# A convolution feeding two MLPs on one Trainium2 core: an instruction order written out in full, with the convolution moved to the second MLP's stretches

## The chip, the cores and the metric

The kernel runs on one core of one Trainium2 chip. The metric is the time of one execution in microseconds (us) of device time; the time before is the median of three runs.

## The reference, cut to what matters

`x` has 4 sequences of 4096 tokens with 192 channels; each of 8 heads (24 channels) has a softmaxed filter of 7 taps. Two MLPs follow, 192 to 2048 to 192, on the 16384 tokens. `x` and the filter come in float32, the MLPs' weights in float64, which the kernel turns into float32 with integer operations.

```python
w = softmax(weight)                        # 8 heads x 7 taps
out = einsum('hk,bskhg->bshg', w, x_unf)   # causal convolution over the tokens
h = out @ w_in1;  z = (h * cos(h)) @ w_out1
h = z @ w_in2;    y = where(h > 0, h, exp(min(h, 0)) - 1) @ w_out2
```

## The kernel before, in words

Channels lie on partitions, tokens in the free dimension. The 16384 tokens are 32 **blocks** of 512, and four blocks make a **group**. A group goes through the first MLP (32 steps, here a *stretch of MLP 1*), then through the second (a *stretch of MLP 2*), so that the activation table changes twice a group. A block has 16 hidden tiles of 128 x 512; a **step** is two of them (`u` and `v`), eight steps a block, 512 steps in all. The list `steps` says which block and which pair comes when; before, the first two blocks of the first stretch are interleaved there with a lag of three steps (`SKEW`).

Each number is split into a high and a low part, and products are made of high x low, low x high and high x high. A step has these parts:

- `emit_A` (L501, matmuls L509): 18 matmuls of 64 rows make `u` and `v` in PSUM; two matmuls, one on each half of the array's rows, run at a time. PSUM has two buffers for `u`, two for `v`.
- For each of the two tiles an element chain. MLP 1: `emit_act1` (ACT L517, the whole number of turns), `emit_mid` (DVE L528, the fraction), `emit_act2` (ACT L534, sine), `emit_g` (DVE L542, the product). MLP 2: ACT L519, ACT L536, DVE L544. The last of them frees the PSUM buffer. Then `emit_hi` (ACT L550, `gh`) and `emit_lo` (POOL L555, `gl`) split the result.
- `emit_B` of the step two before (`LAG`, L558, matmuls L574, in the first two blocks L571): 20 matmuls of 64 rows into four accumulators `a0, b0, a1, b1`, which have one buffer each. At a block's end `evac` (L576) empties them: ACT copies two (L587), DVE two (L591), and `sums` (L597) adds the pairs on POOL (L602, L606), folds a half onto the other (ACT L604, POOL L608), and splits the result for MLP 2 (ACT L612, L615, POOL L614, L617) or transposes and stores it (DVE L628, L631).

`element(q)` (L748) writes one tile at a time: sine of tile q-1, first ACT operation of tile q, product of q-1, `mid` of q, split of tile q-2.

Three streams are fed in between the steps, each a generator that is called a number of times per step:

- `convs()` (L687): the convolution of the coming blocks, for the 128 lower channels (`"a"`) of each block and for the 64 upper channels (`"c"`) of two blocks at once. One `conv` (L334) is eight calls with one DVE operation each: a transpose (L342), a first tap (L354), six more taps (L356, with two inputs in SBUF). Block 0's upper channels and block 1 are made by TensorE (`conv_by_products`, L395, matmuls L405). Three buffers hold its results for the lower channels (`YA`).
- `prepare()` (L636): the decoding of both MLPs' weights. An item of 128 x 256 numbers is a load, ACT and DVE operations (L178 to L184), an add on POOL (L186), and a split (ACT L218 or L239, POOL L220 or L241). `need` (L681) drives it until the weights that a step wants are there.
- `chores`: `sums`, `begin_split` (L721, the split of the next block's convolution, which first drives `convs()` until that block is there) and `double_z`, one call at each half of a step.

In `step` (L766) `convs()` is called once a step in MLP 1 and twice in MLP 2, but not where a chore has run. The order of the first 48 steps (`FREE`) is set by a scheduler, from there on the code's order is the engines' order.

## Time and profile before

| | |
|---|---|
| runs | 2497.09, 2501.37, 2496.46 us (median 2497.09) |
| profiled execution | 2503.75 us, its span 2502.0 us |
| PE busy | 2368.6 us (95%), weight loads 1948.2 us (78%) |
| ACT busy | 1886.8 us (75%) |
| POOL busy | 1735.9 us (69%) |
| DVE busy | 1626.5 us (65%) |
| mean granted TensorE clock | 0.970 |

The first row is what a change is measured by; the second belongs to the one execution from which all rows of the trace come. A busy share is a mean over stretches of different kinds, so it is read stretch by stretch. Matmuls overlap their neighbours, so the time from one matmul's start to the next one's start says more than one matmul's length. "Idle before" is the time that an engine stood still just before an instruction, with what ended it.

### The profile page before, as it was taken

The numbers are of one execution on the slowest core, as the hardware profiler recorded it, in microseconds if no ns is written. First come the engines' busy times: TensorE is split into PE (matmuls) and PEld (weight loads), VectorE is DVE, ScalarE is ACT, GpSimd is POOL, SyncE is SP. The second block draws the span as 40 slices with busy tenths as digits, with TensorE's granted clock in tenths as the row PEclk, the third lists the DMA queues.
The fourth block names the chain that finished last, engine by engine and source line by source line (L and its number), as shares of the span: only waits on it lengthen the run. The fifth ranks groups of instructions, "written<-read, shape, count | busy, mean of one in ns | idle before, by whom it ended". The sixth has DMA issues, their size and how long they took to land.

```text
span 2502.0 us, 51010 instructions
## 1 busy us (share of the span) xinstructions
PE 2368.6 (95%) x19426; PEld 1948.2 (78%) x19426; DVE 1626.5 (65%) x2341; ACT 1886.8 (75%) x3527; POOL 1735.9 (69%) x1395
## 2 busy tenths in 40 slices
PE   7987999899999999999999999999999999999998
PEld 4655888788887888878887788787887878887886
DVE  8689456776567755776557865677556775577533
ACT  5565878678787787777777787777878777777876
POOL 6467777567776677666777677767766767766775
PEclk8797999999999999999999999999999999999999
DMA  5023121211221122212121212121122112211111
GB/s 157 5 60 100 32 46 33 55 41 24 59 53 24 41 47 43 47 27 57 34 59 25 63 24 53 37 47 41 26 57 53 24 40 53 43 35 38 31 31 31
DMA packets 279782, 112.14 MB, mean 45 GB/s; under 512 B 231920, under 2 KB 246512, under 8 KB 279536
## 3 DMA queue, kind: packets, MB, share of 16 engines
q1 hardware_dynamic: 279216, 108.62, 20.1%
q8 instruction: 152, 2.49, 0.4%
q14 instruction: 94, 0.77, 0.1%
q10 hardware_dynamic: 320, 0.26, 0.0%
HBM read 30.18 MB, written 12.58 MB: 17 GB/s over the span
## 4 chain that ended last, share of the span: by engine, by line
PE 61%; DVE 19%; ACT 8%; POOL 4%; issue 4%; DMA 1%; SPq 1%; POOLq 0%; DVEq 0%; ACTq 0%
PE a L574 28%; PE u L509 25%; DVE y L356 6%; DVE w L528 5%; DVE w L542 4%; PE v L509 4%; PE b L574 3%; ACT w L534 3%; POOL gl L555 2%; ACT w L517 1%; ACT w L536 1%; ACT w L519 1%; ACT gh L550 1%; DVE y L354 1%; PE a L571 1%
## 5 line engine op out<-in xcount | busy, mean ns | idle before, releaser
L555 POOL TENSOR_TENSOR gl<-w,gh 128x512 fp32r<-128x512 f32 x1024 | 1347.2, 1320 | 701.0 <-ACT gh L550 564.6
L574 PE MATMUL a<-gh,wo_hl 64*128 64x512 f32 x1984 | 620.4, 393 | 66.3 <-ACT w L534 37.7
L550 ACT ACTIVATE gh<-w 128x512 fp32r<-128x512 f32 x1024 | 640.2, 626 | 22.7 <-DVE w L542 13.4
L574 PE MATMUL b<-gh,wo_hl 64*128 64x512 f32 x1984 | 620.2, 393 | 0.4 <-DVE e L591 0.3
L574 PEld LDWEIGHTS a<-gh,wo_hl 64*128 64x128 f32 x1984 | 365.9, 186 | 137.6 <-ACT w L534 48.4
L534 ACT ACTIVATE w<-w 128x512 f32<-128x512 f32 x512 | 321.6, 630 | 175.0 <-DVE w L528 173.8
L544 DVE SCALAR_TENSOR_TENSOR w<-w,u 128x512 f32<-128x512 f32 x256 | 176.1, 688 | 409.2 <-ACT w L536 399.7
L509 PE MATMUL u<-ch,wi_c 64*128 64x512 f32 x1024 | 404.1, 395 | 0.0
L509 PE MATMUL v<-ch,wi_c 64*128 64x512 f32 x1024 | 403.0, 394 | 0.7
L574 PE MATMUL a<-gl,wo_hl 64*128 64x512 f32 x992 | 395.6, 399 | 8.2 <-POOL gl L555 7.3
L509 PE MATMUL u<-sh,wi_o 64*128 64x512 f32 x1024 | 400.8, 391 | 1.7 <-DMA sh<-xh 1.7
L509 PE MATMUL v<-sh,wi_o 64*128 64x512 f32 x1024 | 400.4, 391 | 0.0
L574 PE MATMUL b<-gl,wo_hl 64*128 64x512 f32 x992 | 394.9, 398 | 0.0
L574 PE MATMUL a<-gh,wo_s 64*128 64x512 f32 x992 | 389.4, 393 | 0.0
L574 PE MATMUL b<-gh,wo_s 64*128 64x512 f32 x992 | 388.9, 392 | 0.0
L574 PE MATMUL a<-gl,wo_s 64*128 64x512 f32 x992 | 388.2, 391 | 0.0
L574 PE MATMUL b<-gl,wo_s 64*128 64x512 f32 x992 | 387.9, 391 | 0.0
L574 PEld LDWEIGHTS b<-gh,wo_hl 64*128 64x128 f32 x1984 | 365.0, 186 | 10.9 <-DVE e L591 0.7
L536 ACT ACTIVATE w<-w 128x512 f32<-128x512 f32 x512 | 318.7, 626 | 0.9
L356 DVE SCALAR_TENSOR_TENSOR y<-xT,wch,y 128x512 f32<-128x512 f32 x276 | 308.2, 1117 | 1.6
L519 ACT ACTIVATE w<-u 128x512 f32<-128x512 f32 x256 | 152.7, 596 | 173.6 <-PE v L509 117.2
L544 DVE SCALAR_TENSOR_TENSOR w<-w,v 128x512 f32<-128x512 f32 x256 | 176.0, 687 | 127.1 <-ACT w L536 121.7
(150 smaller groups left out, 7207.3 us busy)
## 6 DMA issues: line engine op xcount, KB each, us to landing
out_dram<-e SPq DMA_DIRECT2D x192, 64.0 KB, 1.9
xa<-in_x_dram SPq DMA_DIRECT2D x112, 88.0 KB, 2.7
sh<-xh SPq DMA_DIRECT2D x64, 128.0 KB, 2.4
sl<-xl SPq DMA_DIRECT2D x64, 128.0 KB, 2.3
cl<-zc SPq DMA_DIRECT2D x64, 128.0 KB, 2.3
ch<-zc SPq DMA_DIRECT2D x64, 128.0 KB, 2.4
sl<-zl SPq DMA_DIRECT2D x64, 128.0 KB, 2.3
sh<-zh SPq DMA_DIRECT2D x64, 128.0 KB, 2.3
```

The source lines that it names most:

```text
L354: nc.vector.tensor_scalar(out=o, in0=i, scalar1=w, scalar2=None, op0=ALU.mult)
L356: behind[0] = nc.vector.scalar_tensor_tensor(out=o, in0=i, scalar=w, in1=o, op0=ALU.mult, op1=ALU.add).ins
L509: led[0] = nc.tensor.matmul(u[i], lhsT=at, rhs=x[k + h][p], start=n == 0, stop=n == len(ops) - 1).ins
L519: nc.scalar.activation(out=w, in_=u, func=AF.Relu, scale=-1.0)
L528: paced[0] = nc.vector.scalar_tensor_tensor(out=w, in0=u, scalar=0.25, in1=w.bitcast(I32), op0=ALU.add, op1=ALU.subtract).ins
L534: nc.scalar.activation(out=w, in_=w, func=AF.Sin, scale=6.283185)
L536: nc.scalar.activation(out=w, in_=w, func=AF.Exp, scale=-1.0)
L542: nc.vector.tensor_tensor(out=w, in0=u, in1=w, op=ALU.mult)
L544: paced[0] = nc.vector.scalar_tensor_tensor(out=w, in0=w, scalar=-1.0, in1=u, op0=ALU.add, op1=ALU.max).ins
L550: nc.scalar.activation(out=gh, in_=wrk[s], func=AF.Copy)
L555: nc.gpsimd.tensor_tensor(out=gl, in0=wrk.pop(s), in1=f32(gs[s][0]), op=ALU.subtract)
L574: nc.tensor.matmul(a[o + i], lhsT=w[p, f, :], rhs=g[p], start=first, stop=final)
```

## The change

1. **Element steps two tiles at a time.** The function `element` goes. A step writes `act1` of both tiles, `mid` of both, then twice: split of one tile of the step before, `act2` and `g` of one tile of this step.
2. **Convolution in MLP 2's stretches alone.** `convs()` is called twice in each step of MLP 2, whether or not a chore has run, and not in MLP 1 (a third call in each step of the first group's MLP 2 stretch, once the weights are decoded). A fourth buffer holds the lower channels' results, so that a whole group's convolution can be made ahead. Blocks 2 and 3 of the first group are made by TensorE (lower channels).
3. **Blocks in single file.** The interleaving of blocks 0 and 1 goes, and with it their matmuls of 128 rows (L571).
4. **Decoding by step.** The decoding is called four times in each of the first eight steps, then once a step. Its first ACT operation is always ACT's for MLP 1 (before, every other time DVE's). During the first eight steps one PSUM bank holds a tile of the decoding, so that `v` has one buffer there.
5. **Accumulators.** ACT copies `a0` and `a1`, and DVE adds `b0` and `b1` to the copies as it reads them from PSUM; the two adds on POOL (L602, L606) go.
6. No order is set by a scheduler any more.

```diff
-            both = 2 if (m, b0) == (1, 0) else 0
-            if both:
-                for j in range(NP + SKEW):
-                    steps += [(m, b, j - b * SKEW) for b in range(both) if 0 <= j - b * SKEW < NP]
-            steps += [(m, b, j) for b in range(b0 + both, b0 + GROUP) for j in range(NP)]
+            steps += [(m, b, j) for b in range(b0, b0 + GROUP) for j in range(NP)]
...
-        u = [ps_h.tile([P, N], F32, tag=f"u{i}", name="uv"[i]) for i in (0, 1)]
+        spare_bank = banks and s % 2 == 0
+        u = [ps_h.tile([P, N], F32, tag="u0", name="u"), (banks[0] if spare_bank else ps_h).tile([P, N], F32, tag="u1", name="v", bufs=1)]
...
-        for i in (1, 3):
-            if a[i] is not None:
-                nc.scalar.activation(out=e[i], in_=a[i], func=AF.Copy, scale=scale)
-        yield
...
+        for i in (0, 2):
+            nc.scalar.activation(out=e[i], in_=a[i], func=AF.Copy, scale=scale)
+        yield
+        for i in (0, 2):
+            nc.vector.scalar_tensor_tensor(out=e[i], in0=a[i + 1], scalar=scale, in1=e[i], op0=ALU.mult, op1=ALU.add)
+        chores.append(sums(m, b, e))
+        yield
...
+        for b in range(ROWS, NBLK):
+            while b - GROUP not in split_done:
                 yield
             yield from conv("a", b)
-            if b >= ROWS and b % 2 == 0:
+            if b % 2 == 0:
                 yield from conv("c", b)
             conved.add(b)
...
     def step(s):
...
+        if s == NP:
+            need(1, NF, "oh", "os")
+            top.close()
+            banks.append(ctx.enter_context(tc.tile_pool(name="ps_u", bufs=1, space=bass.MemoryType.PSUM)))
+        pair_of = lambda k: (2 * k, 2 * k + 1) if 0 <= k < total else ()
+        now, old = pair_of(s), pair_of(s - 1)
+        calls = 0 if prepared else CALLS if s < NP else 1
+        if now:
             m, b, j = steps[s]
             need(m, j + 1, 0, 1, "c")
             emit_A(s)
-        element(2 * s, None)
+        for q in now:
+            emit_act1(q)
+        for q in now:
+            emit_mid(q)
...
         for i in (0, 1):
-            if i:
-                element(2 * s + 1, finish)
-            next(prep, None)
-            if not chore():
-                if s < FREE:
-                    with tc.issue_after(paced[0]):
-                        next(cq, None)
-                elif s >= total or steps[s][0] == 2 or i == 0:
-                    next(cq, None)
+            if calls > i:
+                next(prep, None)
+            if old:
+                emit_hi(old[i])
+                emit_lo(old[i])
+            if now:
+                emit_act2(now[i])
+            next(finish, None)
+            if now:
+                emit_g(now[i])
+            busy = chore()
+            if s < NP:
+                for _ in range(EARLY // 2):
+                    next(cq, None)
+            elif len(conved) < GROUP or s >= total or steps[s][0] == 2:
+                next(cq, None)
+        for _ in range(calls - 2):
+            next(prep, None)
+        if prepared and NP * GROUP <= s < 2 * NP * GROUP:
+            next(cq, None)
```

Where the order moves. First, DVE in the fourth stretch of MLP 1, eleven steps before its end (`w<-u,w` and `w<-v,w` at L528/L524 are `mid` of the two tiles, at L542/L538 the products; L356 is a tap of the convolution, L460/L463 the split of the next block). Before:

```order
L528 SCALAR_TENSOR_TENSOR w<-u,w 128x512
L356 SCALAR_TENSOR_TENSOR y<-xT,wch,y 128x512 x5
L342 STREAM_TRANSPOSE xT<-xa 128x704
L542 TENSOR_TENSOR w<-u,w 128x512
L528 SCALAR_TENSOR_TENSOR w<-v,w 128x512
L460 TENSOR_TENSOR xl<-y,xh 128x512
L542 TENSOR_TENSOR w<-v,w 128x512
```

Now:

```order
L524 SCALAR_TENSOR_TENSOR w<-u,w 128x512
L524 SCALAR_TENSOR_TENSOR w<-v,w 128x512
L538 TENSOR_TENSOR w<-u,w 128x512
L463 TENSOR_TENSOR xl<-y,xh 128x512
L538 TENSOR_TENSOR w<-v,w 128x512
```

Five taps and a transpose stood between a tile's `mid` and its product; no operation of the convolution is left there, and the two `mid` stand together.

Second, ACT in the step of the same stretch that empties the accumulators (`e<-b` or `e<-a` is the copy out of an accumulator, `gh<-w` the split). Before:

```order
L517 ACTIVATE w<-u 128x512
L550 ACTIVATE gh<-w 128x512
L534 ACTIVATE w<-w 128x512
L517 ACTIVATE w<-v 128x512
L587 ACTIVATE e<-b_14035 128x512
L587 ACTIVATE e<-b_14037 128x512
L550 ACTIVATE gh<-w 128x512
L534 ACTIVATE w<-w 128x512
```

Now:

```order
L515 ACTIVATE w<-u 128x512
L515 ACTIVATE w<-v 128x512
L546 ACTIVATE gh<-w 128x512
L530 ACTIVATE w<-w 128x512
L574 ACTIVATE e<-a_14159 128x512
L574 ACTIVATE e<-a_14161 128x512
L546 ACTIVATE gh<-w 128x512
L530 ACTIVATE w<-w 128x512
L585 ACTIVATE e<-e 64x512
```

Between `mid` of a tile and its sine (L534/L530) ACT now has the other tile's first operation and a split to do; the copy of the half (L585) follows in the same step, since it no longer waits for POOL.

Third, DVE in a step of MLP 2 that empties the accumulators (L591 reads one accumulator, L577 adds one to ACT's copy of the other). Before:

```order
L544 SCALAR_TENSOR_TENSOR w<-w,u 128x512
L591 TENSOR_SCALAR e<-a_15058 128x512
L591 TENSOR_SCALAR e<-a_15060 128x512
L544 SCALAR_TENSOR_TENSOR w<-w,v 128x512
L544 SCALAR_TENSOR_TENSOR w<-w,u 128x512
```

Now:

```order
L540 SCALAR_TENSOR_TENSOR w<-w,u 128x512
L347 STREAM_TRANSPOSE xT<-xa 128x704
L577 SCALAR_TENSOR_TENSOR e<-b_15163,e 128x512
L577 SCALAR_TENSOR_TENSOR e<-b_15165,e 128x512
L540 SCALAR_TENSOR_TENSOR w<-w,v 128x512
L358 TENSOR_SCALAR y<-xT,wch 128x512
```

An operation of the convolution now stands ahead of the reads that free the accumulators, and another behind the second tile's product.

## Rows read from the trace of the kernel before

**Rows 1.** The page's first part: busy time and share of each engine.

```profile
PE 2368.6 (95%) x19426; PEld 1948.2 (78%) x19426; DVE 1626.5 (65%) x2341; ACT 1886.8 (75%) x3527; POOL 1735.9 (69%) x1395
```

**Rows 2.** Windows by stretch: from:to, us, busy PE PEld DVE ACT POOL, clock, DMA.

```profile
423.30:585.90 162.60, 145.69 (x1222) 128.30 (x1218) 127.25 (x174) 117.84 (x217) 105.94 (x83) 0.96 0.19 38
...
1021.50:1178.80 157.30, 147.62 (x1222) 125.99 (x1218) 118.78 (x162) 118.03 (x216) 105.62 (x83) 0.97 0.16 35
1178.80:1318.00 139.20, 138.54 (x1216) 113.32 (x1216) 75.69 (x110) 111.03 (x211) 102.12 (x79) 1.00 0.25 50
...
2202.40:2355.90 153.50, 145.26 (x1214) 121.36 (x1212) 108.89 (x154) 118.00 (x216) 105.41 (x83) 0.98 0.17 38
```

**Rows 3.** Timeline of DVE and PE where a block ends; last row, a tap elsewhere.

```profile
1059.04 1.74 DVE L356 SCALAR_TENSOR_TENSOR y<-xT,wch,y 128x512 f32<-128x512 f32 x1
1061.90 1.27 DVE L591 TENSOR_SCALAR e<-a 128x512 f32<-128x512 f32 x2
1062.72 0.47 PE L574 MATMUL a<-gh,wo_hl 64*128 64x512 f32 x1 [1.79 <-ACT w L534]
1064.30 0.62 PE L574 MATMUL a<-gh,wo_hl 64*128 64x512 f32 x1
1064.73 0.62 PE L574 MATMUL a<-gh,wo_hl 64*128 64x512 f32 x1
...
1206.94 0.75 DVE L356 SCALAR_TENSOR_TENSOR y<-xT,wch,y 128x512 f32<-128x512 f32 x1
```

**Rows 4.** Timeline of DVE and PE at the five taps in a row.

```profile
1117.82 4.84 DVE L356 SCALAR_TENSOR_TENSOR y<-xT,wch,y 128x512 f32<-128x512 f32 x5
1124.90 0.61 PE L574 MATMUL a<-gh,wo_hl 64*128 64x512 f32 x1 [2.87 <-ACT gh L550]
```

**Rows 5.** Groups by line in the MLP 1 stretch 1021.5 to 1178.8 (busy us, mean ns).

```profile
L356 DVE SCALAR_TENSOR_TENSOR y<-xT,wch,y 128x512 f32<-128x512 f32 x17 | 23.8, 1401 | 0.1
L528 DVE SCALAR_TENSOR_TENSOR w<-u,w 128x512 f32<-128x512 f32 x31 | 21.2, 684 | 4.6 <-ACT w L517 4.2
L587 ACT ACTIVATE e<-b 128x512 f32<-128x512 f32 x8 | 4.3, 596 | 0.0
L536 ACT ACT_TABLE_LOAD x1 | 1.3, 1283 | 0.0
```

**Rows 6.** The same in the MLP 2 stretch 1178.8 to 1318.

```profile
L555 POOL TENSOR_TENSOR gl<-w,gh 128x512 fp32r<-128x512 f32 x65 | 85.9, 1325 | 38.6 <-ACT gh L550 31.3 <-issue 4.8 <-PE b L574 1.5
L356 DVE SCALAR_TENSOR_TENSOR y<-xT,wch,y 128x512 f32<-128x512 f32 x19 | 16.9, 891 | 0.0
```

**Rows 7.** Windows of the first group: steps 0-2, 3-7, 8-15, 16-23, 24-31, 32-39, 40-63.

```profile
26.50:76.20 49.70, 40.04 (x127) 23.98 (x125) 44.33 (x83) 30.67 (x74) 38.17 (x46) 0.77 0.27 79
76.20:110.20 34.00, 34.00 (x128) 23.78 (x129) 14.40 (x22) 18.29 (x35) 12.69 (x12) 0.78 0.00 1
110.20:158.50 48.30, 44.92 (x239) 31.72 (x238) 35.98 (x56) 33.38 (x61) 28.87 (x24) 1.00 0.21 55
158.50:237.10 78.60, 55.96 (x321) 40.60 (x321) 74.00 (x122) 44.65 (x95) 56.24 (x59) 0.81 0.30 84
237.10:276.40 39.30, 36.27 (x273) 27.81 (x271) 24.85 (x42) 31.44 (x59) 29.13 (x27) 0.91 0.26 53
276.40:312.80 36.40, 35.93 (x300) 29.34 (x298) 12.96 (x20) 30.33 (x56) 27.51 (x22) 1.00 0.11 25
312.80:417.80 105.00, 104.31 (x914) 89.69 (x912) 57.47 (x83) 81.65 (x154) 74.14 (x57) 1.00 0.23 45
```

**Rows 8.** The same windows for the decoding's line L183 alone (one per item).

```profile
26.50:76.20 49.70, 10.37 (x20) 0.77 0.27 79
...
158.50:237.10 78.60, 8.73 (x20) 0.81 0.30 84
```

**Rows 9.** Groups by line over the span: the convolution on TensorE, all 128 rows.

```profile
L405 PE MATMUL y<-rows 128*128 128x512 f32 (+1 forms) x8 | 5.8, 878 | 0.0
```

**Rows 10.** Windows: the first eight steps of the stretch that starts at 1021.5.

```profile
1021.50:1058.20 36.70, 35.24 (x312) 31.32 (x310) 28.66 (x41) 28.61 (x54) 24.97 (x20) 1.00 0.19 40
```

More of the change, by code (lines that the diff above doesn't have):

```diff
@@ L22 @@
 GROUP = 4
-HID = 2
 LAG = 2
@@ L304, in from_rows @@
         p = slice(0, D2 if alone else P)
[L305 removed]
+        ps = [ps_a.tile([P, N], F32, tag=ACC[i], name="xps") if b < 2 and (alone or b == 1) else ps_h.tile([P, N], F32, tag="u0", name="xps") for i in range(2)]
         for o, k0, c, np in ((ps[0], KM, KH, 2 * Q), (ps[1], 0, KM, P)):
@@ L332, in from_rows, with y_tile @@
         return xT
+    def y_tile(what, b):
+        if what == "a" and b >= GROUP and b % GROUP == GROUP - 1:
+            return later[0].tile([P, N], F32, tag="y", name="y")
+        return yp.tile([P, N], F32, tag="y" + what, name="y", bufs=YA if what == "a" else 2)
     def conv(what, b):
@@ L406, in conv_by_products @@
             yield
+        if what == "a" and b > 1:
+            y = y_tile(what, b)
+            nc.scalar.activation(out=y, in_=o, func=AF.Copy)
+            o = y
         ys[what, b] = o
     xTs = {}
-    behind = [None]
-    tiled = [True]
-    def one_by_one():
-        return tc.issue_after(behind[0]) if behind[0] is not None and tiled[0] else nullcontext()
     def tokens(*order):
@@ L560, in emit_B @@
         h, l, sel = (wo[m, n] for n in ("h", "l", "s"))
-        whole = m == 1 and b < 2
         if j == 0:
-            acc[m, b] = [ps_a.tile([P, N], F32, tag=n, name=n) for n in (ACC[b::2] if whole else ACC)]
+            acc[m, b] = [ps_a.tile([P, N], F32, tag=n, name=n) for n in ACC]
         a = acc[m, b]
@@ L820, in conv_then_two_mlps @@
         need(1, 1, 0, 1, "c")
-    for s in range(FREE):
-        step(s)
-    tiled[0] = False
-    with tc.manual_schedule():
-        for s in range(FREE, total + LAG):
+        for s in range(total + LAG):
             step(s)
```

140 lines of the change are left out of this document (49 added, 91 removed).

## The prediction

> **What bounds the kernel now.** The page's first part comes first: PE is busy for 95% of the span, the others for 65 to 75% [rows 1]. A mean over unlike stretches cannot say what 5% of idle PE is worth, so the windows come next, cut where the MLPs change [rows 2]. A stretch of MLP 2 takes 139.2 us with PE busy for 138.5 of them at the full clock: nothing else can bound it. A stretch of MLP 1 has the same 32 steps and takes 162.6, 157.3 and 153.5 us in the rows shown. The seven stretches of MLP 1 and the six of MLP 2 between them fill 423.3 to 2355.9 us, 1932.6 us; with six times 139.2 taken out, the seven take 1097 us, 156.8 each, 18 us above the floor that MLP 2 shows. There PE is idle for 10 us and its mean clock is 0.96 to 0.98.
>
> The timeline says where. At a block's end a tap of the convolution takes 1.74 us on DVE (it overlaps a POOL operation there; the shortest ones take 0.75, last row), the reads that empty the accumulators therefore start at 1061.90, and the next block's first output matmul waits 1.79 us; then pairs of matmuls start 0.43 us apart (1064.30, 1064.73) instead of 0.23, since the clock fell to its lower level [rows 3]. Once a group `begin_split` drives five taps at once, 4.84 us on DVE, and PE stands for 2.87 us [rows 4]. So DVE's order is the bound of MLP 1, not DVE's amount of work. The first group is a case by itself: its 64 steps take 391.3 us, where PE's pace would need 278 [rows 7].
>
> **The change, part by part.** Durations are from the profiled execution, 2503.75 us (span 2502.0, 1.75 around it), which stands 6.7 above the median of the runs; that comes off at the end.
>
> *Stretches of MLP 1, groups 2 to 8.* The 17 taps in the stretch shown cost 23.8 us of DVE [rows 5]. Without them DVE has 95 us of work, ACT still 118, POOL less than 105 (two adds a block go), all under PE's 138.5 [rows 2]. The new order also takes away ACT's wait for `mid`: between a tile's `mid` (0.68) and its sine ACT has another 0.59 and 0.63 us to do. What could still hold PE is the block's end: copies and reads ran side by side, now DVE's add comes after ACT's copy. After the block's last matmul: copy 0.60 [rows 5], add 0.68 (taken from L528, which also reads one operand in PSUM [rows 5]) with 0.1 between them, so the first pair of accumulators is free after 1.4 us and the second after some 2.1. PE has nine pairs of `emit_A` in between, 9 x 0.2275 = 2.05 us (138.5 us / 608 pairs = 0.228), and needs the second pair 0.46 later still. It just fits; I take 0.4 us a block for the operations that may stand ahead of the add, and 1 us for the table load of 1.28 [rows 5]. A stretch then takes 138.5 + 1 + 4 x 0.4 = 141 us, seven take 987: **-110**. Bounds: 139.2 as MLP 2 now (-123), and 36.7 per eight steps, which is what the fastest block end-to-end shows now with three taps in it [rows 10], 147 a stretch (-68).
>
> *Stretches of MLP 2.* 17 taps come in at 0.89 us [rows 6], 15 us, and some four first taps and transposes, at a tap's price 4 more: DVE goes from 75.7 to some 95, far below 138.5. They hide beside PE as the 19 taps there do now. Not hidden is one at a block's end: convolution is now called whether or not a chore runs, so a tap stands ahead of the adds (third place of the order). With 0.75 us ahead, the first pair is free after about 2.2 us and not 1.4, against 2.05: 0.1 to 0.5 us; with 1.74 ahead, 1.1. I take 0.5 us, three times a stretch (the convolution is done after 24 of 32 steps), six stretches: **+9**. Bounds 0 and the second rival. The last stretch has no convolution and stays.
>
> *The first group* [rows 7], by pieces:
> - Steps 0 to 7 take 83.7 us now, 49.7 of them with 20 items of decoding [rows 8] and DVE busy for 44.3. The same items come in the first six steps. To those 44.3 come four operations of 0.68 for each of five more steps (14) and eight of the convolution (7): 65 us, at the same 89% share 73. `v` has one buffer, so a step's matmuls wait for the last product of the step before; I take 80. Bounds 70, and 110 if the clock stays low all through as it does from steps 2 to 5 now (mean 0.77 and 0.78).
> - Steps 8 to 15: 48.3 us now; eight steps at 4.35, seven products of the convolution at 0.88 [rows 9] and 5 us of waits make 46. Bounds 41 and 55.
> - Steps 16 to 31: 117.9 us now, since 20 items fall into seven steps with DVE busy for 74 of 78.6. One call a step makes it 0.6 items a step: DVE needs 2.2 us an item (the 74 less 22 for the elements and some 8 for convolution and splits, over 20), so 4 x 0.68 + 0.6 x 2.2 = 4.05 us a step, just below PE, with POOL and ACT near it too; I take 4.85 a step, 78 us. Bounds 70 and 95.
> - Steps 32 to 39: 36.4 us now. Some ten items are left, and `need` drives them just before the matmuls that use them: 48. Bounds 36 and 58.
> - Steps 40 to 63: 105.0 us now; three operations of the convolution a step for 16 steps make DVE's 4.7 us a step: 109. Bounds 104 and 115.
>
> Together 361 against 391: **-30**, bounds -70 and +42.
>
> Sum: -110 + 9 - 30 = -131; 2503.75 - 131 = 2372.75, less 6.7: 2366, say **2367 us**, for the median.
>
> **The rivals.**
> 1. *MLP 1 keeps half of its loss.* ACT and POOL carry the splits and `sums` in a bunch after each block's end, and 36.7 us stands for eight steps even where PE does not lose its clock. 147 us a stretch, 42 more: 2409. Against it: ACT's 118 us leave 20 free. 14%.
> 2. *The taps cost MLP 2 more.* If each of 36 taps takes 1.74 us as where it meets POOL [rows 3], 24 of 32 steps need 2 x 0.69 + 1.5 x 1.74 + 0.7 = 4.7 us of DVE against 4.33: 9 us a stretch, and the adds at three block ends come 1.3 us late with 1.6 us of low clock behind, 9 more: 6 x 18 less the 9 counted is 99 more, 2466. Against it: at two taps a step the taps there average 0.89 now [rows 6]. 6%.
>    The Trainium skill (SBUF — State Buffer, "Who interferes with whom") says that a VectorE instruction with two SBUF inputs and a GpSimd instruction that reads SBUF share a port, and that whichever comes second is blocked for the other's whole length. Rows 3 agree (1.74 against 0.75 us). By that rule at its worst each tap waits out one whole split of 1.32 us [rows 6], an estimate of 2.07 us a tap, some 20 us a stretch besides the block ends, and the time would be near 2530 (1%, in the last 2% below).
> 3. *The first group grows.* With every piece at its upper bound it is 42 longer, not 30 shorter: 2439. For it: one buffer for `v`, products on PE, low clock. Against it: DVE's bunch in steps 18 to 24 goes. 5%.
> 4. *Slower: the accumulators come free too late.* The one mechanism is copy, then add, then the next block's first matmul. It decides from 2.05 us after the last matmul on: if a wait of 0.7 us or more regularly stands before the add (ACT still in a sine when the block ends, a tap on DVE), PE pays at all 64 block ends what it pays in rows 3: 1.79 idle and eight pairs at 0.2 more, 3.4 us, 218 us in all. Less the 20 counted, 198 more: 2565. Against it: in MLP 1 nothing but products and `mid` stands there. 3%.
>
> That the change doesn't do what it says is excluded for MLP 1 by the order itself: no operation of the convolution stands between its steps. What it can't exclude, 2%.
>
> **How the numbers follow.** The forecast's own case has 70%, within 2335 to 2400 (the bounds of the first group, mostly). The range reaches down to 2325 for a first group at its best, and up to 2430 to take in rival 1 and part of rival 3; that leaves out under 2 in 10. About 0.2%, 5 us, is what a measurement here can tell from no change. Faster: the forecast, rivals 1 and 3 and most of 2, 94%. Same 2%. Slower: rival 4 and a little else, 4%.
>
> **What would show it.** In the changed profile the windows of the seven MLP 1 stretches should be 139 to 143 us, with no gap of PE above 1 us and the clock at 1.00; DVE's busy time should be about 92 to 95 us in either kind of stretch, ACT's wait for `mid` near nothing. The MLP 2 stretches should be 140 to 142 us, with what is lost at the three block ends that have a tap ahead of the adds. The 64 first steps should take some 360 us, the first eight about 80, with the granted clock the doubtful row. Wrong would be a stretch of MLP 1 above 147 us, PE waiting for the adds (L577) at each block's end, or a first group that is no shorter.

## The result, and the profile after

The change takes 2459.14 us in the median of four runs (2452.73 to 2463.16), the kernel before beside it 2497.49 (four runs): a ratio of 0.9841, with an interval from 0.9815 to 0.9867. That is 1.6% faster, where 5.2% were forecast, and outside the range. The profiled execution took 2456.48 us (span 2454.8). Against its counterpart of before, 2503.75, the sum of the prediction stood at 2372.75; so 84 us have to be found.

The page's first part, busy time and share by engine, hardly differs from [rows 1]; GpSimd alone has clearly less to do:

```profile
PE 2342.7 (95%) x19614; PEld 1896.1 (77%) x19614; DVE 1612.3 (66%) x2314; ACT 1860.3 (76%) x3544; POOL 1607.1 (65%) x1273
```

The windows by stretch answer to [rows 2] (from:to, length, busy PE, PEld, DVE, ACT, POOL, granted clock, DMA): a stretch of MLP 1, the stretch of MLP 2 behind it, and the last one of MLP 2, which has no convolution.

```profile
1011.90:1151.30 139.40, 139.25 (x1223) 117.46 (x1221) 92.75 (x140) 114.18 (x216) 95.11 (x74) 1.00 0.15 34
1151.30:1301.50 150.20, 144.93 (x1217) 115.97 (x1215) 102.95 (x132) 111.23 (x210) 97.07 (x71) 0.99 0.26 52
...
2308.40:2442.80 134.40, 133.78 (x1170) 108.80 (x1168) 50.81 (x76) 105.64 (x201) 87.14 (x70) 1.00 0.12 26
```

MLP 1 is at TensorE's pace: 139.4 us, 139.25 of them busy, at the full clock. MLP 2 has become the slow one: 150.2 us, TensorE idle for over 5. The last stretch, 134.4 against 134.1 before, shows that without convolution the new order costs MLP 2 nothing. From the first split of a stretch to that of the next, the seven MLP 1 stretches take 139.7 us in the mean (156.7 before), the six MLP 2 stretches 149.9 (139.3 before).

The blocks of that MLP 2 stretch, in the same columns:

```profile
1151.30:1189.30 38.00, 35.81 (x306) 29.32 (x304) 31.09 (x37) 27.84 (x54) 27.93 (x20) 1.00 0.24 47
1189.30:1225.80 36.50, 35.61 (x307) 28.41 (x305) 28.60 (x37) 26.99 (x52) 23.68 (x17) 1.00 0.32 61
...
1262.40:1301.50 39.10, 37.79 (x308) 29.88 (x306) 20.70 (x31) 29.36 (x55) 23.11 (x17) 0.96 0.24 48
```

Before, the four took 34.9, 34.5, 34.5 and 35.2. Two things happen. The first is at a block's end; the timeline of four engines (start, length, engine, line, in brackets the idle time before and what ended it):

```profile
1196.92 1.74 POOL L587 TENSOR_TENSOR e<-e 64x512 f32<-64x512 f32 x1
1198.63 3.76 POOL L551 TENSOR_TENSOR gl<-w,gh 128x512 fp32r<-128x512 f32 x3
1198.66 4.28 DVE L360 SCALAR_TENSOR_TENSOR y<-xT,wch,y 128x512 f32<-128x512 f32 x1
1199.95 0.49 PE L566 MATMUL a<-gl,wo_hl 64*128 64x512 f32 x1 [0.70 <-POOL gl L551]
1202.86 0.60 ACT L517 ACTIVATE w<-u 128x512 f32<-128x512 f32 x1 [2.37 <-PE v L507]
1202.87 0.68 DVE L540 SCALAR_TENSOR_TENSOR w<-w,u 128x512 f32<-128x512 f32 x1
```

GpSimd does the fold (L587, 1.74 us), and the splits that waited behind it then follow without a pause, three of them in 3.76 us. A tap that starts with the first ends only after the third: 4.28 us, where a tap alone takes 0.75 [rows 3]. The product behind it (L540) comes only at 1202.87. TensorE stands for 0.70 us until the first of the late splits is there, and ScalarE for 2.37 us until TensorE has made the next `v`. A tap of over 4 us stands at 16 of the 18 block ends that have taps in the six MLP 2 stretches, and nowhere else in them. In the whole stretch the group of the taps answers to [rows 6], with 1284 ns in the mean, not 891:

```profile
L360 DVE SCALAR_TENSOR_TENSOR y<-xT,wch,y 128x512 f32<-128x512 f32 x36 | 46.2, 1284 | 0.0
```

The second is in the last block. The timeline of SyncE's queue and of TensorE:

```profile
1283.50 2.81 SPq L252 DMA_DIRECT2D xa<-in_x_dram  x4
1286.41 1.11 SPq L442 DMA_DIRECT2D sh<-xh  x2
1287.57 1.24 SPq L442 DMA_DIRECT2D sl<-xl  x2
1288.86 1.23 SPq L446 DMA_DIRECT2D ch<-ch  x2
1291.20 0.50 PE L507 MATMUL u<-ch,wi_c 64*128 64x512 f32 x1 [0.67 <-DMA ch<-ch]
1292.54 0.50 PE L507 MATMUL u<-cl,wi_c 64*128 64x512 f32 x1 [0.20 <-DMA cl<-cl]
1293.34 0.49 PE L507 MATMUL v<-cl,wi_c 64*128 64x512 f32 x1 [0.30 <-DMA cl<-cl]
1294.42 0.63 PE L507 MATMUL u<-sh,wi_o 64*128 64x512 f32 x1
```

The convolution of the next group starts before this stretch is over, and its four token loads (2.81 us to issue) stand ahead of the swaps that the coming MLP 1 step needs. TensorE waits for `ch` and `cl`, and its matmuls then take 0.63 us each (0.39 at the full clock). The window behind, in the columns above, has a mean granted clock of 0.60: of its 4 us, 3.2 are at the lower level, 1.2 GHz.

```profile
1294.00:1298.00 4.00, 4.00 (x24) 3.19 (x22) 1.29 (x2) 2.84 (x4) 1.12 (x1) 0.60 0.00 0
```

The windows of the first group, cut as [rows 7] (steps 0 to 7 in two pieces, 8 to 15, 16 to 23, 24 to 31, 32 to 39, 40 to 63):

```profile
24.70:75.00 50.30, 36.24 (x171) 20.93 (x172) 28.09 (x61) 33.08 (x78) 30.05 (x37) 0.87 0.30 86
75.00:113.30 38.30, 30.17 (x175) 20.23 (x174) 25.49 (x46) 22.17 (x49) 23.33 (x24) 0.87 0.04 13
113.30:157.90 44.60, 42.29 (x315) 30.66 (x313) 31.81 (x48) 31.98 (x63) 29.64 (x25) 1.00 0.16 40
157.90:206.80 48.90, 39.76 (x309) 30.85 (x307) 36.31 (x59) 31.75 (x65) 31.46 (x29) 0.93 0.21 57
206.80:246.50 39.70, 36.26 (x307) 30.92 (x304) 34.39 (x48) 31.48 (x62) 30.52 (x28) 1.00 0.20 54
246.50:310.90 64.40, 43.76 (x307) 33.87 (x305) 39.91 (x66) 37.34 (x77) 42.54 (x44) 0.84 0.27 65
310.90:426.20 115.30, 109.50 (x915) 91.43 (x913) 94.28 (x119) 82.81 (x156) 71.47 (x51) 0.99 0.32 61
```

401.5 us in all, against 391.3 before. Steps 16 to 31 did gain 29 us (88.6 for 117.9), but steps 32 to 39 lost 28 (64.4 for 36.4) and steps 40 to 63 lost 10. From the list of waits in steps 36 to 39 (engine, line, waited for: us, times, longest), and from the timeline of step 22 (counted from 0; an expectation below calls it step 23):

```profile
PE u L507 <- POOL wi_o L220: 18.8, 3, 10.1
```

```profile
190.82 1.10 SPq L442 DMA_DIRECT2D sl<-xl  x2
194.59 1.33 SPq L198 DMA_DIRECT2D raw<-in_moe_w_in_dram  x2
198.34 0.43 ACT L181 ACTIVATE t<-raw 128x256 f32<-128x256 uint32 x1 [8.70 <-DMA raw<-in_moe_w_in_dram]
```

The second MLP's weights come too late for its first steps; and in step 22 a load of weights stands behind the swaps on SyncE's queue, and ScalarE waits 8.70 us for it.

### The profile page after: what moved, and what is told of

It reads as the page before. It is cut to its first block, busy times and chain, and to the rows that moved or that the text cites. A ratio compares the mean times of both kernels' runs of the same rounds, so it can differ in the third digit from the quotient of the medians.

```text
span 2454.8 us, 51057 instructions
## 1 busy us (share of the span) xinstructions
PE 2342.7 (95%) x19614; PEld 1896.1 (77%) x19614; DVE 1612.3 (66%) x2314; ACT 1860.3 (76%) x3544; POOL 1607.1 (65%) x1273
## 5 line engine op out<-in xcount | busy, mean ns | idle before, releaser
L566 PE MATMUL b<-gh,wo_hl 64*128 64x512 f32 x2048 | 636.2, 391 | 10.4 <-DVE e L577 10.4
L566 PE MATMUL a<-gh,wo_hl 64*128 64x512 f32 x2048 | 638.8, 391 | 5.5 <-ACT gh L546 5.5
L566 PE MATMUL a<-gl,wo_hl 64*128 64x512 f32 x1024 | 409.1, 399 | 20.8 <-POOL gl L551 19.7
L540 DVE SCALAR_TENSOR_TENSOR w<-w,u 128x512 f32<-128x512 f32 x256 | 175.5, 686 | 381.5 <-ACT w L532 378.5
L566 PEld LDWEIGHTS a<-gh,wo_hl 64*128 64x128 f32 x2048 | 381.2, 186 | 57.6 <-ACT gh L546 6.0
L566 PEld LDWEIGHTS b<-gh,wo_hl 64*128 64x128 f32 x2048 | 379.4, 186 | 40.7 <-DVE e L577 18.5
L566 PE MATMUL b<-gl,wo_hl 64*128 64x512 f32 x1024 | 406.3, 397 | 0.0
L566 PE MATMUL b<-gh,wo_s 64*128 64x512 f32 x1024 | 400.0, 391 | 0.0
L515 ACT ACTIVATE w<-u 128x512 int32<-128x512 f32 x256 | 152.5, 596 | 235.0 <-PE v L507 94.4
L530 ACT ACTIVATE w<-w 128x512 f32<-128x512 f32 x512 | 321.6, 628 | 5.1 <-DVE w L524 4.9
L524 DVE SCALAR_TENSOR_TENSOR w<-u,w 128x512 f32<-128x512 f32 x256 | 176.6, 690 | 217.3 <-ACT w L515 217.1
```

What stands on the lines that cost most here:

```text
L515: nc.scalar.activation(out=w.bitcast(I32), in_=u, func=AF.Copy, bias=0.25)
L524: nc.vector.scalar_tensor_tensor(out=w, in0=u, scalar=0.25, in1=w.bitcast(I32), op0=ALU.add, op1=ALU.subtract)
L530: nc.scalar.activation(out=w, in_=w, func=AF.Sin, scale=6.283185)
L540: nc.vector.scalar_tensor_tensor(out=w, in0=w, scalar=-1.0, in1=u, op0=ALU.add, op1=ALU.max)
L566: nc.tensor.matmul(a[o + i], lhsT=w[p, f, :], rhs=g[p], start=first, stop=final)
```

## The experiments

A single run is compared with the 2456.48 us of the changed kernel's profiled execution. The kernel before took between 2493 and 2506 us in the executions beside the experiments, the changed kernel between 2453 and 2463, so that 10 us between two single runs are not read as a difference. Stretches and blocks are measured in the traces as above.

### The last block: what stands on SyncE's queue

Two edits. The first, in `step`, keeps the next group's convolution from starting early:

```diff
-            elif len(conved) < GROUP or s >= total or steps[s][0] == 2:
+            elif len(conved) < GROUP or s >= total or steps[s][0] == 2 and s % (2 * NP * GROUP) < NP * GROUP + 25:
```

> Convolution calls in the second MLP's stretches only during the first 25 of their 32 steps, so that the next group's convolution, and with it the next load of tokens, doesn't start before the last split's swaps. In the changed kernel the last block of six MLP 2 stretches takes 39.1 us against 36.5 for the block before it: SyncE issues four token loads (2.8 us) ahead of sh, sl, ch and cl, TensorE waits for ch, and the clock falls after the wait. Theory (queue on SyncE): the last block falls to 35 to 36.5 us, the low clock at the turn of the stretches is gone, and the time falls by 15 to 25 us to about 2432 to 2442. Rival (the taps, or the split itself, make the last block long): the last block stays within 0.5 us of 39.1 and the time within 5 us of the changed kernel's 2456. The first three blocks stay at 38.0, 36.5 and 36.6 by both.

2423.9 us, 33 less: more than expected. The last blocks take 35.0 us, but the first ones fell too, from 38.0 to 36.4, which neither theory had: the convolution now meets the first block's end at another of its operations. Ahead of the adds (L577) stands one tap of 0.75 us, where the change has taps of 1.79 and 1.48 us and a transpose, and in the stretch that answers to the one above TensorE's wait of 1.05 us for the adds is gone. This edit takes taps out of the last block as well, so the queue alone was tried with a second one, in `conv`:

```diff
+        late = b > ROWS and b % GROUP == 0
-        if n == 0 and ROWS <= b < NBLK - 1:
+        if n == 0 and ROWS <= b < NBLK - 1 and not late:
             load_a(b + 1)
...
                 nc.vector.scalar_tensor_tensor(out=o, in0=i, scalar=w, in1=o, op0=ALU.mult, op1=ALU.add)
+            if n == 0 and k == 3 and late:
+                load_a(b + 1)
             yield
```

> The changed kernel with one thing moved on SyncE alone: at the end of six MLP 2 stretches the four token loads that stood ahead of the swaps sh, sl, ch and cl stand behind them; the order on VectorE, ScalarE, GpSimd and TensorE is the same to the last instruction. Theory (the queue on SyncE makes the last block 39 us): last blocks of 35 to 36.5 us, the first blocks within 1 us of 38.0, and the time 12 to 25 us less than 2456. Rival (what the run without the early start gained came from the taps that left the last block): last blocks of 38 us or more and the time within 6 us of 2456.

2434.2 us, 22 less. The window of the last block of the stretch that answers to the one above, then SyncE's timeline there:

```profile
1253.10:1288.20 35.10, 35.10 (x311) 28.89 (x309) 20.53 (x31) 29.35 (x56) 23.14 (x17) 1.00 0.27 53
```

```profile
1275.82 2.35 SPq L449 DMA_DIRECT2D cl<-cl  x2
1278.57 2.13 SPq L252 DMA_DIRECT2D xa<-in_x_dram  x4
```

TensorE is busy for all of the 35.1 us, at the full clock, and the other three blocks are as they were. The cause is shown for this kernel: four loads at the wrong place of one queue cost some 4 us at a stretch's end. (The sixth of the stretches, behind which there is nothing left to load, has a last block of 35.0 us in the changed kernel already.) The place alone need not cost anything: in the run with single elements below the loads stand ahead of the swaps as well, and the last blocks take 35.5 us; there the split is done 9.3 us ahead of the next stretch's first matmul, here 7.0.

### The block ends: a tap held up by GpSimd

```diff
-                nc.vector.scalar_tensor_tensor(out=o, in0=i, scalar=w, in1=o, op0=ALU.mult, op1=ALU.add)
+                if b < ROWS:
+                    nc.vector.scalar_tensor_tensor(out=o, in0=i, scalar=w, in1=o, op0=ALU.mult, op1=ALU.add)
+                else:
+                    nc.vector.transpose(out=o, in_=i)
```

> From block 4 on the six taps are 32x32 transposes of the same 128x512 tiles on VectorE (0.70 us in the profile of before, one input), in the same places of the order; the sums of the convolution are left out. Theory (port: a tap with two inputs in SBUF is held up by GpSimd's work, up to 4.3 us, and holds up the second tile's g behind it): blocks of six MLP 2 stretches fall from 38.0, 36.5 and 36.6 us to 35 to 35.5, and the time by 6 x 4 to 6 x 6, about 25 to 35 us, to 2421 to 2431 us; the last block falls by no more than 2. Rival (any 0.7 us instruction of VectorE there does the harm, since g waits behind it): blocks stay within 0.5 us and the time within 8 us of 2456.

2421.8 us. Blocks of 35.6 us in place of 38.0, 36.5 and 36.6, and the last one still 39.1, as the theory has it (the blocks 0.1 above what it gave). The fold, too, takes 1.28 to 1.31 us at all block ends of these stretches, where beside the taps it took 1.73 to 1.76: each holds up the other. The instructions by line, all groups from the second on (lowest, median, highest ns), first the taps of the change, then the transposes in their places:

```profile
L360 DVE SCALAR_TENSOR_TENSOR y<-xT,wch,y x210: 698/1170/4329, 572.3 to 2116.8; 128x512 f32<-128x512 f32 x105
```

```profile
L363 DVE STREAM_TRANSPOSE y<-xT x210: 660/697/706, 566.4 to 2080.7; 128x512 f32<-128x512 f32 x105
```

Next, the fold's add on VectorE in MLP 2 (`m == 2`) in place of GpSimd, nothing else:

```diff
-        eng.tensor_tensor(out=e[2][lo], in0=e[2][lo], in1=e[3][lo], op=ALU.add)
+        (nc.vector if m == 2 else eng).tensor_tensor(out=e[2][lo], in0=e[2][lo], in1=e[3][lo], op=ALU.add)
```

> In the second MLP the fold's add (1.75 us on GpSimd, ahead of the next lo's) goes to VectorE; nothing else changes. Theory (the tap is starved by three or four GpSimd operations in a row, one of them the fold): the longest taps fall from 4.3 us to below 2.5, blocks of MLP 2 from 36.5 to 35 to 36, the time by 8 to 25 us to 2431 to 2448. Rival (GpSimd's lo's alone are enough, or VectorE is now the one that is late): blocks at 36.3 to 37.5, the time within 6 us of 2456 or above.

2433.9 us. The second and third block take 35.3 us, so it is the fold that makes GpSimd's run at those two block ends. The first stays at 38.0 and has taps of 4.3 us still: the block that ends there is the last one of MLP 1 (`m == 1`), whose fold the edit leaves on GpSimd. From the timeline there:

```profile
1153.19 1.75 POOL L587 TENSOR_TENSOR e<-e 64x512 f32<-64x512 f32 x1
1156.60 4.33 DVE L360 SCALAR_TENSOR_TENSOR y<-xT,wch,y 128x512 f32<-128x512 f32 x1
```

The second block's window:

```profile
1182.30:1217.60 35.30, 35.19 (x307) 28.50 (x305) 26.68 (x38) 27.06 (x52) 23.32 (x16) 1.00 0.33 63
```

Then the one point of the old rule that the change had dropped: no call of the convolution where a chore has run.

```diff
-            elif len(conved) < GROUP or s >= total or steps[s][0] == 2:
+            elif len(conved) < GROUP or s >= total or steps[s][0] == 2 and not busy:
```

> Convolution still only in the second MLP's stretches, but not in the half of a step that has a chore (the rule of before on this one point). The run with taps in both MLPs had MLP 2 blocks of 35.5 us and differs from this one by a call a step in MLP 1's steps. Theory (a tap next to a chore, at the block's end, is what costs): blocks of MLP 2 fall from 38.0, 36.5 and 36.6 to 35 to 35.8 while MLP 1 stretches stay at 139.4 to 140.5; with the last block still at 38 to 39 the time is 2425 to 2440. Rival (two calls a step in the second MLP are too many, wherever they stand): blocks stay at 36.3 or above and the time within 8 us of 2456.

2492.3 us: neither. In MLP 2 the blocks behind the first fall as the theory says (35.5, the last one 35.6). The first stays at 37.7 in the mean, without any tap above 1.76 us: taps of 1.75 and 1.48 us still stand ahead of the adds (no chore runs there yet), and TensorE waits 1.94 us for them in the stretch looked at. And the calls no longer suffice for a group's convolution, and `begin_split` drives what is missing inside MLP 1, whose stretches rise to 152 us from the third group on. A window of one, and from the timeline its six taps in a row and the wait behind them:

```profile
1007.10:1159.30 152.20, 144.31 (x1220) 120.29 (x1218) 106.05 (x156) 114.08 (x217) 95.08 (x75) 0.97 0.20 43
```

```profile
1059.40 4.69 DVE L360 SCALAR_TENSOR_TENSOR y<-xT,wch,y 128x512 f32<-128x512 f32 x6
1066.29 0.79 PE L566 MATMUL a<-gh,wo_hl 64*128 64x512 f32 x1 [3.55 <-ACT gh L546]
```

That is the picture of [rows 4] again. So the unconditional calls are the price for keeping MLP 1 clean, unless the missing ones go elsewhere. A try at that, on top of the run with three edits (the last section here):

```diff
-            elif len(conved) < GROUP or s >= total or steps[s][0] == 2:
+            elif len(conved) < GROUP or s >= total:
                 next(cq, None)
+            elif steps[s][0] == 2 and not busy and s % (2 * NP * GROUP) < NP * GROUP + 25:
+                for _ in range(1 + (s % NP in (0, 6, 7))):
+                    next(cq, None)
```

> As the run before it (fold on VectorE, decoding twice a step, no call of the convolution after the 25th step of an MLP 2 stretch), but a step half that has a chore calls no convolution, and the first and the two last steps of a block call it twice in each such half, so that the 36 taps of a group still all fall into its MLP 2 stretch. Theory (a tap is only dear next to chores and GpSimd's run at a block's end): the longest tap falls from 4.3 us to 2 or less, the first block of an MLP 2 stretch from 36.4 to 35.5, the others stay at 35.2, and the time is 3 to 8 us below the run before it. Rival (four calls a step make VectorE late in the middle of the block): MLP 2 blocks of 35.5 us or more, and the time 5 us or more above it.

2464.9 us (0.9862 of before, 0.9848 to 0.9877), 78 above the run it was to improve on: the rival. No tap is longer than 1.8 us now, and still the MLP 2 stretches take 152.8 us, with first three blocks of 37.6 to 40. Four calls in a step make VectorE late where it had been in time; the length of the longest tap is not what counts by itself. The calls of a block's first step now stand ahead of the adds, and in the stretches behind the first group TensorE waits for those (us, times, longest):

```profile
PE b L566 <- DVE e L577: 36.8, 21, 2.4
```

That is the mechanism of the prediction's rival 4; in the run it was to improve on the same wait is 1.7 us.

### What made MLP 1 faster

Five runs undo parts of the change: the place of the taps, the order of the elements, the block end. Taps in both MLPs by the old rule:

```diff
-            elif len(conved) < GROUP or s >= total or steps[s][0] == 2:
+            elif len(conved) < GROUP or s >= total or not busy and (steps[s][0] == 2 or i == 0):
```

> The rule of before for convolution calls, in the changed kernel: one call a step in either MLP's stretches, two in the second MLP's, and none in a step half that has another chore. All else stays as changed. Theory A (the MLP 1 stretches are shorter, 140 us against 157, because the taps left them): they go back to 150 us or more, the MLP 2 stretches fall to 140 to 146, and the time rises by 20 to 60 us. Rival B (the two-tile order of the element steps made them shorter, and it can take taps): MLP 1 stretches stay at or below 145 us, MLP 2 stretches fall by 4 us or more each, and the time falls by 5 us or more.

Elements one at a time from the second group on (`element` as before):

```diff
+        if s >= SWITCH:
+            now = old = ()
+            element(2 * s, iter(()))
...
+            if i and s >= SWITCH:
+                element(2 * s + 1, finish)
```

> From the second group on the element steps go one tile at a time in the order of before (sine of the last tile, first pass of this one, product, mid, then the split of the tile before the last); the convolution stays out of MLP 1, and the block end stays copy and add. Theory A (the order in pairs is what made the MLP 1 stretches 17 us shorter, as the run with taps in both, 143.3 us, suggests): MLP 1 stretches rise from 139.6 to 148 us or more, and the time to 2510 or more. Rival B (the taps' absence is enough): they stay at or below 143 us and the time is within 25 us of 2456.

Both edits together:

> From the second group on, the element order of before (one tile at a time) and the convolution in both MLPs by the rule of before; only the block end stays that of the change (copy on ScalarE, then add on VectorE, no adds on GpSimd). Pairs with taps in MLP 1 gave 143.3 us for its stretches, single file without taps 141.6, both together absent gave 139.6, before 156.8. Theory A (taps and the old order are dear only together, since then a tap delays the pass that ScalarE waits for): MLP 1 stretches of 150 us or more, the time 2500 or more. Rival B (the block end was the cause: reads by two engines and GpSimd's adds): MLP 1 stretches at or below 146 us, the time at or below 2460.

The block end of before in the changed kernel:

```diff
-        for i in (0, 2):
+        for i in (1, 3):
             nc.scalar.activation(out=e[i], in_=a[i], func=AF.Copy, scale=scale)
         yield
         for i in (0, 2):
-            nc.vector.scalar_tensor_tensor(out=e[i], in0=a[i + 1], scalar=scale, in1=e[i], op0=ALU.mult, op1=ALU.add)
+            nc.vector.tensor_scalar(out=e[i], in0=a[i], scalar1=scale, scalar2=None, op0=ALU.mult)
...
+        eng.tensor_tensor(out=e[2], in0=e[2], in1=e[3], op=ALU.add)
+        yield
         nc.scalar.activation(out=e[3][lo], in_=e[2][hi], func=AF.Copy)
+        eng.tensor_tensor(out=e[0], in0=e[0], in1=e[1], op=ALU.add)
```

> The changed kernel with the block end of before: ScalarE copies two accumulators, VectorE reads the other two, GpSimd adds them (two adds more a block); pairs, and the convolution in MLP 2 alone, stay. Theory A (the block end was not what cost MLP 1 its 17 us): MLP 1 stretches at or below 142 us. Rival B: 146 us or more. MLP 2 stretches rise by both, since GpSimd's run at the block end is longer and a tap meets it: by 2 to 10 us.

And old order with old block end, so that from the second group on only the taps have moved:

> From the second group on, the element order of before and the block end of before; only the convolution stays in MLP 2 alone. This is the change with nothing but the move of the taps. Theory A (the taps were the cause in MLP 1, as the prediction had it): MLP 1 stretches at or below 144 us, at least 13 of the 17 us. Rival B (the block end): 150 us or more. MLP 2 stretches of 139.2 us before, now with 36 taps and not 19: 141 to 146.

Mean lengths (us) of the seven MLP 1 and the six MLP 2 stretches, with the time of the run:

| elements | taps in MLP 1 | block end | MLP 1 | MLP 2 | time |
|---|---|---|---|---|---|
| single (before) | 17 a stretch | old | 156.7 | 139.3 | 2503.8 |
| single | 10 to 12 | new | 149.1 | 139.3 | 2452.9 |
| pairs | 10 to 12 | new | 143.4 | 143.5 | 2437.3 |
| single | none | old | 143.4 | 146.7 | 2462.9 |
| pairs | none | old | 141.8 | 149.0 | 2468.9 |
| single | none | new | 141.6 | 144.1 | 2435.8 |
| pairs (the change) | none | new | 139.7 | 149.9 | 2456.5 |

Windows of the MLP 1 and the MLP 2 stretch of the run with nothing but the taps moved, and the MLP 1 window of single elements with taps and the new end:

```profile
1014.70:1158.00 143.30, 141.50 (x1217) 114.78 (x1215) 95.17 (x143) 117.21 (x217) 104.27 (x83) 1.00 0.15 34
1158.00:1304.30 146.30, 142.22 (x1222) 126.11 (x1220) 97.92 (x129) 111.54 (x210) 108.91 (x79) 1.00 0.27 53
```

```profile
1001.30:1150.60 149.30, 144.34 (x1218) 119.30 (x1216) 112.96 (x156) 117.31 (x217) 94.62 (x75) 0.99 0.20 44
```

In the first of them TensorE stands for under 2 us; in the last, with the taps in, for 5, and VectorE has 113 us of work instead of 95. Moving the taps alone gives 13.3 of the 17.0 us (its theory A); the order and the block end are worth 1.6 and 1.8 more on top of it. But pairs and the new block end with 10 to 12 taps left in MLP 1 give 13.3 as well (143.4; the rival B of that run), and single elements without taps give 15.1 (rival B again): the causes overlap, and no one of them has the 17 us to itself. With taps in MLP 1 the order in pairs is worth 5.7 (149.1 to 143.4). The run of both edits (149.1) fell between its two theories; it has fewer taps than before and none in a row (so has the run with pairs), so it doesn't price the block end alone. The old block end left the MLP 2 stretches as they were (149.0 for 149.9), against what was expected of it.

The table's other half: every run without taps in MLP 1 pays for them in MLP 2, 5 to 11 us a stretch (146.7 with nothing else changed, just above the 141 to 146 expected). Old order and old rule in MLP 2 cost nothing (139.3). Net of both, the new place of the taps is worth nothing here: with pairs and the new end, taps in both MLPs give 2437.3, taps in MLP 2 alone 2456.5.

### The first group

```diff
-        calls = 0 if prepared else CALLS if s < NP else 1
+        calls = 0 if prepared else CALLS if s < NP else 2
```

> After the eighth step decoding is called twice a step instead of once. In the changed kernel steps 37 to 39 take 16.6, 11.1 and 12.3 us, since TensorE waits for the second MLP's first weights (wi_o, 18.8 us in all), and step 23 takes 12.2. Theory (one call a step is too few, and the rest of the decoding falls into four steps): steps 36 to 39 fall from 44.8 us to 20 to 26, steps 16 to 31 rise by no more than 8 (88.6 now), and the time falls by 10 to 22 us to 2434 to 2446. Rival (the loads behind the swaps on SyncE set the pace, more calls don't help): steps 36 to 39 stay above 40 us or what they gain is lost in steps 16 to 31, and the time is within 5 us of 2456.

2442.7 us, 14 less. The windows of steps 16 to 31 and 36 to 39:

```profile
164.60:261.60 97.00, 80.86 (x602) 60.18 (x600) 88.06 (x138) 69.32 (x144) 76.83 (x75) 0.95 0.29 72
283.10:301.20 18.10, 17.82 (x157) 15.03 (x155) 17.96 (x20) 12.67 (x25) 15.07 (x11) 1.00 0.41 83
```

Steps 36 to 39 take 18.1 us for 45.2, better than expected; steps 16 to 31 lose 8.4 and steps 8 to 15 another 6, so half of it is given back, with VectorE busy for 88 of 97 us.

```diff
-        if m == 1:
+        turn[0] += 1
+        if m == 1 and turn[0] % 2:
             nc.scalar.activation(out=size, in_=f32(hi), func=AF.Abs)
```

> Decoding of the first MLP's weights takes every second absolute value on VectorE, as before the change, and no longer all of them on ScalarE. Steps 0 to 7 take 88.6 us in the changed kernel against 83.7 before; VectorE waits 21.5 us there for ScalarE's t (L181). Theory A (ScalarE is the late engine of the first steps): steps 0 to 7 fall by 3 to 8 us. Rival B (VectorE's work is the bound, as the prediction had it): they rise by 2 us or more. Elsewhere nothing changes, so the time is within 8 us of 2456 by both.

2463.6 us. Steps 0 to 7 take 95.4 us, not 88.6, with VectorE busy for 57.7 of them, not 53.6: rival B by its number. But VectorE stands idle for 40% of the time, so it isn't its amount of work that binds here; which wait does was not settled. The granted clock is also lower there, 0.79 for 0.87, and TensorE busy for 73.1 us in place of 66.4, as much more as the steps are longer; in the other runs, with the same code there, they take 88.7 to 91.9.

### What helps, put together

> No early start of the next group's convolution, and the second MLP's fold on VectorE, together. Alone they gave 2424 and 2434 us. If they are separate causes (the queue on SyncE for the last block and the first, GpSimd's run of operations ahead of a tap for the others), blocks are 36 or less, 35.3, 35.3 and 35, a stretch of MLP 2 141 to 142 us, and the time is 2424 less 6 x 2.5, about 2406 to 2412. Rival (both cut the same wait): the time stays within 5 us of 2424.

2400.0 us: 56 less, the sum of the two (33 and 23), and less than the expected 2406 to 2412. With two calls of decoding:

> No early start of the next group's convolution, the second MLP's fold on VectorE, and two calls of decoding a step after the eighth. The first two together gave 2400 us; the third alone gave 14 (steps 36 to 39 fell by 27 us, steps 8 to 35 rose by 13). Theory (separate places of the program, so they add): 2383 to 2392 us, MLP 2 stretches 141 to 143 us, MLP 1 stretches 139 to 140, the first 64 steps some 388 us. Rival (the fold on VectorE meets the decoding's VectorE work in the first MLP 2 stretch and gives it back): 2395 or more.

2387.4 us (2386.9 to 2388.1), 0.9548 of before (0.9532 to 0.9564). And with the MLP 2 stretches from the second group on in single file:

> The version with three edits that took 2387 us, and from the second group on the MLP 2 stretches' elements one tile at a time, MLP 1's in pairs. Single file gave MLP 2 stretches of 144.2 us where pairs gave 150.3, with nothing else changed. Theory (with a product between two taps the second tile's does not wait for a run of taps): MLP 2 stretches fall from 141.3 to 139.3 to 141, the time to 2375 to 2386. Rival (fold on VectorE and the later start have already taken that gain): 141.3 or more and 2387 or more.

2380.1 us (2378.0 to 2381.4), **0.9526 of before** (0.9498 to 0.9553), which beats both kernels. Its windows of an MLP 1 and an MLP 2 stretch:

```profile
976.20:1114.90 138.70, 138.62 (x1217) 119.94 (x1215) 94.19 (x143) 113.91 (x216) 94.00 (x74) 1.00 0.17 37
1114.90:1255.70 140.80, 139.61 (x1223) 115.00 (x1221) 95.15 (x133) 111.93 (x212) 94.42 (x68) 1.00 0.26 52
```

Its longest tap takes 1.86 us, where the run before it still had some of 4.3.

## Why the prediction was right and wrong

The direction, and the first term, were right. Against the sum, MLP 1 came out 9 us better, MLP 2 54 worse and the first group 40 worse, together the 84 to within 1. **MLP 1**: 141 us were forecast, 139.7 came. The reason given holds in part: moving the taps is enough for 13.3 of 17.0 us, but pairs and the new block end reach as much with most of the taps left in, so that it isn't shown to which of them the change owes it. ScalarE's wait for `mid` went as forecast, from 173.8 us in the whole run to 4.9; where the taps alone moved it is still 116.0 in the stretches, and they take 143.4, so that it was worth little. The block end that "just fits" does fit: ScalarE's copies begin at 1047.74, VectorE's two adds at 1048.49 and end at 1049.77, and TensorE waits for none of it. The timeline:

```profile
1047.74 1.09 ACT L574 ACTIVATE e<-a 128x512 f32<-128x512 f32 x2
1048.49 1.28 DVE L577 SCALAR_TENSOR_TENSOR e<-b,e 128x512 f32<-128x512 f32 x2
```

So rivals 1 and 4 are out for MLP 1.

**MLP 2** is the step that failed: "I take 0.5 us, three times a stretch", +9 in all, where the six stretches came to 899 us, 63 more than the 836 of before. TensorE's waits in the stretches behind the first group (who waited for what: us, times, longest):

```profile
PE a L566 <- POOL gl L551: 15.3, 21, 1.4
PE b L566 <- DVE e L577: 7.2, 6, 1.9
PE u L507 <- DMA ch<-ch: 4.5, 5, 1.1
```

The second is the wait that the sum priced, for the adds: 7.2 us, at one block end of a stretch and not at three. The first and the third it had at nothing: splits that come late from GpSimd, and swaps that come late from SyncE's queue. The waits are not the whole loss (in the stretch of 150.2 us TensorE is idle for 5 of the 11 us; behind a wait its matmuls start farther apart), so the 63 are parted by the runs, into three. With transposes in place of the taps the first three blocks take 106.8 us for 111.3 (4.5 a stretch, 27 us): that is the taps and GpSimd holding each other up, the adds' wait at the first block's end included. Those 106.8 are still 2.6 above the 104.2 of before (16 us). The last stretch, with no operation of the convolution, takes 104.4 for its first three blocks, so nearly all of this is what short instructions in those places cost, the part that the sum's 9 comes nearest to. And the last blocks, 38.5 us in the mean for 35.2, are 20 us of SyncE's queue, on which the prediction laid no price: it counted where the convolution's VectorE operations went, and not the loads that they issue.

For the taps the evidence was at hand and misread. The 0.89 us that a tap took in MLP 2 [rows 6] was kept as a property of the stretch. It belonged to the rule that called no convolution beside a chore; with that rule back, in MLP 2 or in both, the longest tap is 1.85 us and the blocks between the first and the last take 35.3 to 35.5. The prediction noted that the rule goes and went on using the average measured under it. Rival 2 had the right place, the block ends, and came out at 2466, 7 us from the result. That nearness is luck: it put 108 us on MLP 2, where 63 came, and left the first group 30 us shorter, where it is 10 longer. It got 6%, and even its worst case, a tap that waits out one whole split (2.07 us), stays below the 4.28 measured.

The Trainium skill (SBUF — State Buffer, "Who interferes with whom") says that a VectorE instruction with two SBUF inputs contends with a GpSimd instruction that reads SBUF, and that one with at most one SBUF input, outside the modes that use both of VectorE's port pairs, does not. The traces agree with both: 698 to 4329 ns for 210 taps, 660 to 706 for 210 transposes in the same places. By its rule that the second to come waits until the first is done, an estimate gives a tap one split more here, 1.25 us (3.76 us for three); measured were three GpSimd operations, 3.53 us more, and the measurement decides.

**The first group** came to 401.5 us, not 361, and is no shorter than before, the third of the prediction's own signs of being wrong; of its five pieces one was right (steps 8 to 15: 44.6 for 46).
- Steps 0 to 7: 88.6 for 80. The 65 us of VectorE were 53.6, and no engine was near its limit; a share of 89% was carried over to an order that doesn't bind by shares.
- Steps 16 to 31: 88.6 for 78, some 7 of the difference in step 22 behind SyncE's swaps (12.2 us where most steps take 4 to 5). Read in the trace; an order of that queue without it was not tried.
- Steps 32 to 39: 64.4 for 48, past the upper bound of 58. "`need` drives them just before the matmuls" was right, the price was not: an item at that point passes through load, three engines and a split with nothing beside it.
- Steps 40 to 63: 115.3 for 109, the block ends again: in the run with taps in both MLPs and none beside a chore it is 106.4.

The range failed with its terms: up to 2430 it took in most of the first group's bounds, but MLP 2's bound, rival 2 itself, was left outside, with 6% on it.

## What to carry to other kernels

An average read from a trace holds under the rules that made that order: if the change drops a rule, the number goes with it. When work is moved, follow each of its instructions onto every queue it touches, the DMA issues first of all; here four of them at a stretch's end cost 20 us in all. Fillers are best kept from the places where another engine is about to work without a pause, but only as many as fit between the pipeline's own operations: four in a step cost 78 us, more than the meeting's 27.

## What the runs showed of the hardware

A VectorE instruction with two inputs in SBUF that meets GpSimd at work isn't merely delayed by the one operation that it meets: the tap above started 0.03 us after the first of three splits in a row and ended 0.55 us after the last, 4.28 us for 0.75. In 210 places a one-input instruction of the same size was never longer than 706 ns. The hold runs both ways: GpSimd's fold beside the taps took 1.73 to 1.76 us, and 1.28 to 1.31 where transposes stood in their places. And short waits of TensorE cost more than they last: at the turn of the stretches, waits of 0.67, 0.20 and 0.30 us were followed by 3.2 us at the lower clock, and the block took 39.1 us; without the loads ahead of the swaps it took 35.1, at 1.00.
